# Pooled attention into a mixture-of-depths layer: stores on ScalarE's queue, exponentials in token order, and batch 0's dense work moved ahead of batch 2

## Chip, cores and metric

One Trainium2 chip, one core. The time is device microseconds of one execution of the whole program. Engines are called TensorE (PE, with PEld for its weight loads), VectorE (DVE), ScalarE (ACT), GpSimd (POOL) and SyncE (SP); SP only issues DMAs in this kernel.

## What is computed

Eight batches, eight heads, 576 tokens, head dimension 64. Keys and values are averaged over groups of 8 tokens, so each token attends to 72 pooled keys. The heads side by side give x with 512 columns. A gate score per token picks the 128 best tokens of each batch, and only these go through a two-layer network that is added to x.

```python
def _attn_ref(q, k, v):                       # (8, 8, 576, 64)
    k_p = k.reshape(B, H, Sp, pool, D).mean(axis=3)     # pool = 8, Sp = 72
    v_p = v.reshape(B, H, Sp, pool, D).mean(axis=3)
    scores = np.matmul(q, k_p.transpose(0, 1, 3, 2)) / np.sqrt(D)
    attn = softmax(scores)
    return np.matmul(attn, v_p)               # then (B, S, H*D) = x

def _moe_ref(x, w_gate, w1, w2, capacity):    # w1 (512, 1024), w2 (1024, 512), capacity 128
    scores = np.einsum('bsd,d->bs', x, w_gate)
    out = x.copy()
    for b in range(B):
        top_idx = np.argpartition(-scores[b], capacity)[:capacity]
        xe = x[b, top_idx]
        ye = np.maximum(xe @ w1, 0.0) @ w2
        g = 1.0 / (1.0 + np.exp(-scores[b, top_idx]))
        out[b, top_idx] = x[b, top_idx] + g[:, None] * ye
    return out
```

## The kernel before

`direct_path` does all of the work; `general_path` runs afterwards only if a flag says that a softmax sum left its allowed range. The program's order is written out by hand: every engine executes its instructions in the order in which the Python code emits them, and semaphores hold an instruction until its inputs are there and its buffer is free.

**Tiles.** A token's position in a batch is split as 16 groups of 36 (`G`, `TG`). A tile is 64 tokens: 4 positions of each of 16 groups. A batch has 9 tiles, 3 to a *row* of work: row `u` belongs to batch `u // 3`. `q_trans(u)` transposes the queries of a row on VectorE. `scores(u)` fills four PSUM banks on TensorE (32 products, L281) and ScalarE takes the exponential of each bank into `et` (L285). `attend(a)` multiplies with the pooled values for a *chunk*, two tiles in 128 partitions (L294), into a `pA` buffer, of which there are two; column `D` gives the softmax sum and column `D+1` the gate score. `norm(a)` divides on VectorE (L303, L311, L314) into `xs`, which holds two chunks and has two buffers, or `xh` for the last, half-sized columns of a batch. Tiles are numbered through the batches, so with 9 per batch chunk 4 holds the last tile of batch 0 and the first of batch 1.

**Per batch.** `pool_k` and `pool_v` add groups of 8 on GpSimd (L216, L217, L237 to L241), `k_trans` transposes the sums on VectorE (L222 to L228) and `gate_v` reduces the product of pooled values and gate weights (L245). Batch 0 is pooled partly on VectorE. Then comes the routing: `score` (L354 to L358, with five small GpSimd operations), `row_bcast` (L371) which puts all scores on every partition in PSUM, `count` (L382 to L387) which counts larger scores on VectorE, `one_hot` (L394 to L397), and `gather` (L405 to L415): a product that yields token numbers, the index on GpSimd, and an indirect DMA on GpSimd's queue that reads the chosen rows of `out` back from memory. The gather therefore waits for all stores of its batch. `x_trans` transposes the rows (L428) and ScalarE copies them to `xg` (L430); `hidden`, in three parts (L440), and `finish`, in three parts (L452), are the dense products, followed on GpSimd by the sum with x (L454) and, after the third part, an indirect store.

**Order.** `at(u, slot, job)` enters a job in a table, and the loop over `u` runs the slots of a row between attention steps: attend, slot 1, `scores(u + 1)`, the rest of attend, slot 2, norm, `q_trans(u + 2)`, slots 3 to 7. For batch b, with `w = 3(b + 1)`, the routing stands in rows w and w+1, `x_trans` in slot 5 of row w+2, and the six dense parts in slots 4 and 6 of rows w+3 to w+5:

```python
        at(w, 1 if last else 3, row_bcast, b)
        at(w + 1, 5, gather, b, 3)
        at(w + 2, 5, x_trans, b, 2)
        at(w + 3, 4, hidden, b, 0, 2)
        at(w + 5, 6, finish, b, 2, 1)
```

Loads of keys, values and queries run two batches ahead and are issued on SP. So are the stores of x (`store_x`, L331 to L348), one row after their chunk, in the same queue:

```python
            ins = nc.sync.dma_start(out=rows, in_=x)
            others(ins, b, (scat, gath))
```

The output pattern of a full store is `t g (i d)`, with 8 in front, and that of a half-sized one `t g d`, with 4 in front. Constants for routing (`ident`, `before`, `auxb` and others) are made on VectorE by `constants()` in slot 3 of row 0, behind the first normalisation. `bank(i, shape)` names one of four PSUM banks by hand.

Of the kernel before, what the change touches and what calls it, by code (L numbers as in the profile page):

```python
# [48 lines left out]
def direct_path(ctx, tc, q, k, v, moe_w_gate, moe_w1, moe_w2, moe_capacity, out, flag):  # L49
# [20 lines left out]

    nc = tc.nc
# [23 lines left out]
    NCH = B * NT // 2  # L95
# [21 lines left out]

    nc.vector.memset(vraws[0], 0.0)
    nc.gpsimd.memset(vraws[1], 0.0)
# [10 lines left out]
    load_q(0)  # L130
    load_v(0, 0)
# [23 lines left out]
    for t in kts + vps + vraws[2:]:  # L155
        nc.gpsimd.memset(t, 0.0)
    diff = counted("diff", [C, C], [[1, C]], 0, -1)
    part = counted("part", [C, 1], [[0, 1]], 0, 1)
    steps = counted("steps", [C, C // G - 1], [[-G, C // G - 1]], -G, 1)
# [17 lines left out]
    def constants():  # L177
        nc.vector.tensor_scalar(ident, diff, 0.0, None, op0=OP.is_equal)
        nc.vector.tensor_scalar(before[:, NC - 2, :], diff, 0.0, None, op0=OP.is_lt)
        nc.vector.memset(ones, 1.0)  # L180
        nc.vector.memset(one32, 1.0)

        ge, q16, q4, hi = (const.tile([C, n], FT, name=x) for x, n in (
            ("ge", C // G - 1), ("q16", 1), ("q4", 1), ("hi", 1)))
        nc.vector.tensor_scalar(ge, steps, 0.0, None, op0=OP.is_ge, op1=OP.add, accum_out=q16)
        nc.vector.tensor_scalar(q4, q16, 4.0, None, op0=OP.mult)
        nc.vector.scalar_tensor_tensor(hi, q16, -float(G), part, op0=OP.mult, op1=OP.add)
        nc.vector.tensor_scalar(hi, hi, float(TG), None, op0=OP.mult)
        for i, a in enumerate(auxb):
            nc.vector.tensor_scalar(a[:, 0 : NC - 1, 0], numbers, 0.0, hi, op0=OP.mult, op1=OP.add)  # L190
            nc.vector.tensor_copy(a[:, NC - 1, 0:1], hi)
            nc.vector.tensor_scalar(a[:, i : i + NC - 1, 1], numbers, q4, None, op0=OP.add)  # L192
            h = (NC - 1) * (1 - i)
            nc.vector.tensor_scalar(a[:, h, 1:2], q16, float(32 - 4 * i), None, op0=OP.add)
# [10 lines left out]
    def bank(i, shape):  # L205

        return psum.tile(shape, FT, name=f"bank{i}", bufs=1)
# [22 lines left out]
    def pool_v(b, g, eng):  # L230
        x = VR[b, g]
        VP[b] = vps[b % 2]
        h = slice(HG * g, HG * g + HG)
        if eng is nc.vector:
            eng.tensor_reduce(out=VP[b][:, h, 0:D], in_=x.rearrange("p h t d -> p h d t"), axis=AX.X, op=OP.add)
        else:
            eng.tensor_tensor(out=x[:, :, 0:4, :], in0=x[:, :, 0:4, :], in1=x[:, :, 4:8, :], op=OP.add)  # L237
            eng.tensor_tensor(out=x[:, :, 0:2, :], in0=x[:, :, 0:2, :], in1=x[:, :, 2:4, :], op=OP.add)  # L238
            eng.tensor_tensor(out=VP[b][:, h, 0:D], in0=x[:, :, 0, :], in1=x[:, :, 1, :], op=OP.add)

        nc.gpsimd.tensor_tensor(out=x[:, :, 2, :], in0=VP[b][:, h, 0:D], in1=wg[:, h, :], op=OP.mult)  # L241
# [5 lines left out]


# [25 lines left out]
    def scores(u):  # L274
        b = u // NTH
        p = [bank(i, [128, 2, TS * TL]) for i in range(4)]
# [7 lines left out]
        for i in range(4):  # L284
            nc.scalar.activation(ET[u][i], p[i], AF.Exp, scale=exp_scale)  # L285

    def attend(a, heads=range(H)):
        if heads[0] == 0:
            PA[a] = psum.tile([C, 2, 512], FT, name="pA")
        for h in heads:  # L290
            g, n = divmod(h, HG)
            for t in range(2):
                u, i = divmod(2 * a + t, TS)
                nc.tensor.matmul(PA[a][TL * t : TL * t + TL, g, E * n : E * n + E],  # L294
                                 ET[u][h // 2][:, h % 2, TL * i : TL * i + TL], VP[u // NTH][:, h, :],
                                 start=True, stop=True)

    def norm(a):
        o = PA.pop(a)[:, :, 0 : HG * E].rearrange("p g (n d) -> p g n d", d=E)
        rz = rzall[:, a, :].rearrange("p (g n) -> p g n", g=2)  # L300
        if a % NT == 0:
            SS[a // NT] = work.tile([C, NT, H], FT, name="ss")
        nc.vector.reciprocal(rz, o[:, :, :, D])  # L303
        k = a % NT
        if k == NC - 1:
            XS[a] = work.tile([C, 1, DM], FT, name="xh")
        elif k - (k >= NC) in (0, 2, 4, 6):
            XS[a] = work.tile([C, 2, DM], FT, name="xs")
        else:
            XS[a] = XS[a - 1]  # L310
        nc.vector.tensor_tensor(out=XS[a][:, 0 if XS.get(a - 1) is not XS[a] else 1, :].rearrange("p (g n d) -> p g n d", g=2, d=D), in0=o[:, :, :, 0:D],  # L311
                                in1=rzall[:, a, :].rearrange("p (g n one) -> p g n one", g=2, one=1).to_broadcast(
                                    [C, 2, HG, D]), op=OP.mult)
        nc.vector.tensor_tensor(out=SS[a // NT][:, a % NT, :].rearrange("p (g n) -> p g n", g=2),  # L314
                                in0=o[:, :, :, D + 1], in1=rz, op=OP.mult)
# [15 lines left out]
    def store_x(a):  # L331
        def put(b, rows, x):
            ins = nc.sync.dma_start(out=rows, in_=x)
# [3 lines left out]
        b = 2 * (a // NT)  # L337
        k = a % NT
        if k == NC - 1:
            x = XS[a][:, 0, :]  # L340
            for n in range(2):
                put(b + n, out[b + n].rearrange("(g t) d -> t g d", g=G)[32:TG], x[TL * n : TL * n + TL])
        elif XS.get(a - 1) is XS[a]:
            b += k >= NC
            i = (k - 1) % NC if k < NC else k - NC - 1
# [571 lines left out]
```

## Time and profile before

| | |
|---|---|
| median of 3 runs | 268.03 us (267.51 to 274.88) |
| profiled execution, its own time | 272.41 us |
| span of that execution, first to last instruction | 270.6 us |
| mean granted TensorE clock | 0.925 |
| moved by DMA | 46.94 MB, mean 173 GB/s |

| group of instructions | count | mean | busy |
|---|---|---|---|
| scores, TensorE L281 | 768 | 380 ns | 46.6 us |
| attention times values, TensorE L294 | 1152 | 241 ns | 49.0 us |
| `hidden`, TensorE L440 | 512 | 277 ns | 60.5 us |
| `finish`, TensorE L452 | 384 | 311 ns | 60.2 us |
| exponential, ScalarE L285 | 96 | 495 ns | 39.4 us |
| first value sum, GpSimd L237 | 15 | 2354 ns | 35.3 us |
| normalisation, VectorE L311 | 32 | 691 ns | 22.1 us |

The page's first part gives the busy time of each engine, the second cuts the span into 40 slices of 6.77 us: a digit is the busy share in tenths, PEclk the granted TensorE clock in tenths, DMA the mean share of the 16 DMA engines. A table of stages has the length of the stage, then the busy time and the number of instructions for PE, PEld, DVE, ACT and POOL, then the granted clock, the DMA share and GB/s. The chain of waits has start, length and what was waited for. A timeline row has start, length, engine, line, operation, output, inputs and count; engines with a q are the instruction queues of that engine.

### The profile page before, as it was taken

How to read it: one execution, taken by the hardware profiler on the slowest of the kernel's cores; microseconds unless marked ns; L12 is line 12 of the kernel's file. 1: busy time of each engine (PE TensorE's matmuls, PEld its weight loads, DVE VectorE, ACT ScalarE, POOL GpSimd, SP SyncE). 2: the span in 40 equal slices, each digit the busy share in tenths (PEclk: the TensorE clock that was granted, in tenths of full speed). 3: DMA queues.
4: the chain of work that ended last, by engine and by line, in shares of the span. 5: the costliest groups of instructions: out<-in, count | busy, mean ns of one | idle time of the engine just before them, and what ended most of it. 6: DMA issues, size and time to landing. Idle time of an engine off the chain costs nothing.

```text
span 270.6 us, 7289 instructions
## 1 busy us (share of the span) xinstructions
PE 223.3 (83%) x3050; PEld 207.3 (77%) x3050; DVE 137.6 (51%) x387; ACT 66.5 (25%) x162; POOL 155.1 (57%) x193
## 2 busy tenths in 40 slices
PE   0396176680699999999999999999999999999970
PEld 0376165580599799889997998899889999999970
DVE  7859936664064537654755476538554733411000
ACT  2042022211033133323332333223322331212210
POOL 9889706967970229973995299639953103313021
PEclk9999669656589999999999999999999999999995
DMA  7999997876702636686736276831222203301101
GB/s 278 344 354 398 398 354 284 323 274 204 277 13 50 236 88 206 226 263 208 271 65 249 79 217 224 267 95 44 48 71 79 80 18 116 104 2 39 41 0 51
DMA packets 13048, 46.94 MB, mean 173 GB/s; under 512 B 1104, under 2 KB 1104, under 8 KB 10960
## 3 DMA queue, kind: packets, MB, share of 16 engines
q1 hardware_dynamic: 11728, 42.21, 46.1%
q0 software_dynamic: 1280, 4.20, 4.7%
q8 instruction: 26, 0.43, 0.7%
q14 instruction: 14, 0.11, 0.1%
HBM read 34.87 MB, written 11.53 MB: 171 GB/s over the span
## 4 chain that ended last, share of the span: by engine, by line
PE 69%; DVE 13%; DMA 8%; issue 4%; POOL 3%; ACT 0%; POOLq 0%; DVEq 0%
PE bank L452 21%; PE bank L440 18%; PE bank L281 14%; PE pA L294 13%; DMA out_dram<-xs 5%; DVE qt L271 3%; DMA xr<-out_dram,idx 3%; DVE oh L397 2%; PE bank L371 2%; PE bank L428 2%; DVE xs L311 1%; DVE auxb L192 1%; DVE vp L203 1%; PE bank L405 1%; DVE ge L386 1%
## 5 line engine op out<-in xcount | busy, mean ns | idle before, releaser
L281 PE MATMUL bank<-qt,kt 32*128 32x192 f32 x768 | 46.6, 380 | 18.3 <-DVE qt L271 11.7
L440 PE MATMUL bank<-xg,w 128*128 128x128 f32 x512 | 60.5, 277 | 0.0
L452 PE MATMUL bank<-w,ht 128*128 128x176 f32 (+1 forms) x384 | 60.2, 311 | 0.0
L285 ACT ACTIVATE et<-bank 128x384 f32<-128x384 f32 x96 | 39.4, 495 | 81.9 <-PE bank L281 81.9
L440 PEld LDWEIGHTS bank<-xg,w 128*128 128x128 f32 x512 | 58.4, 192 | 0.5 <-ACT et L285 0.5
L452 PEld LDWEIGHTS bank<-w,ht 128*128 128x128 f32 x384 | 55.8, 190 | 0.6
L294 PEld LDWEIGHTS pA<-vp,et 128*64 128x64 f32 x1152 | 42.4, 152 | 15.7 <-issue 14.9
L281 PEld LDWEIGHTS bank<-qt,kt 32*128 32x128 f32 x768 | 38.6, 216 | 20.6 <-POOL sc L168 11.2
L294 PE MATMUL pA<-vp,et 128*64 128x66 f32 x1152 | 49.0, 241 | 6.1 <-DVE rzall L303 4.7
L303 DVE RECIPROCAL rzall<-pA 128x8 f32<-128x8 f32 x36 | 7.5, 207 | 80.3 <-PE pA L294 80.3
L237 POOL TENSOR_TENSOR vraw<-vraw 128x1024 f32<-128x1024 f32 x15 | 35.3, 2354 | 0.9 <-DVE qt L271 0.9
L454 POOL TENSOR_TENSOR y<-y,xr 128x176 f32<-128x176 f32 (+1 forms) x24 | 13.1, 548 | 39.4 <-ACT y L453 39.0
L271 DVE STREAM_TRANSPOSE qt<-qraw 128x512 f32<-128x512 f32 (+1 forms) x48 | 24.5, 551 | 0.0
L442 ACT ACTIVATE ht<-bank 128x384 f32<-128x384 f32 (+1 forms) x24 | 10.9, 456 | 51.9 <-PE bank L440 51.9
L311 DVE TENSOR_TENSOR xs<-pA,rzall 128x512 f32<-128x512 f32 x32 | 22.1, 691 | 1.4 <-DVE rzall L303 0.2
L453 ACT ACTIVATE y<-bank,g 128x176 f32<-128x176 f32 (+1 forms) x24 | 9.7, 403 | 51.2 <-PE bank L452 51.2
L409 POOL TENSOR_SCALAR idx<-tok 128x1 int32<-128x1 f32 x8 | 1.9, 244 | 31.6 <-DVE g L411 31.4
L238 POOL TENSOR_TENSOR vraw<-vraw 128x512 f32<-128x512 f32 x15 | 19.1, 1272 | 1.2
L386 DVE SCALAR_TENSOR_TENSOR ge<-bank,sc,before 128x128 bf16<-128x128 f32 (+3 forms) x40 | 18.2, 498 | 1.6 <-PE bank L371 1.6
L216 POOL TENSOR_TENSOR kraw<-kraw 128x1152 f32<-128x1152 f32 x7 | 18.4, 2634 | 0.1
L362 POOL CAST auxb<-sc 128x5 bf16<-128x5 f32 x8 | 1.6, 202 | 21.1 <-DVE sc L358 10.7
L428 PE MATMUL bank<-ident,xr 128*128 128x128 f32 x32 | 5.3, 292 | 9.2 <-DMA xr<-out_dram,idx 9.2
(85 smaller groups left out, 186.0 us busy)
## 6 DMA issues: line engine op xcount, KB each, us to landing
kraw<-in_k_dram SPq DMA_DIRECT2D x8, 1152.0 KB
qraw<-in_q_dram SPq DMA_DIRECT2D x8, 1152.0 KB
vraw<-in_v_dram SPq DMA_DIRECT2D x16, 512.0 KB
out_dram<-xs SPq DMA_DIRECT2D x16, 512.0 KB
w<-in_moe_w_dram SPq DMA_DIRECT2D x2, 2048.0 KB
vraw<-in_v_dram SPq DMA_DIRECT2D x16, 64.0 KB
out_dram<-xh SPq DMA_DIRECT2D x8, 128.0 KB
wg<-in_moe_w_gate_dram SPq DMA_DIRECT2D x1, 256.0 KB
```

Source lines behind the costliest of these rows:

```text
L216: eng.tensor_tensor(out=x[:, :, 0:2, :], in0=x[:, :, 0:2, :], in1=x[:, :, 2:4, :], op=OP.add)
L237: eng.tensor_tensor(out=x[:, :, 0:4, :], in0=x[:, :, 0:4, :], in1=x[:, :, 4:8, :], op=OP.add)
L238: eng.tensor_tensor(out=x[:, :, 0:2, :], in0=x[:, :, 0:2, :], in1=x[:, :, 2:4, :], op=OP.add)
L271: nc.vector.transpose(out=QT[u][:, :, n : n + m, :].rearrange("p j t c -> p t j c"), in_=x)
L281: nc.tensor.matmul(p[i][:, s, :], KT[b][r, j, s, :], QT[u][r, j, :, G * s : G * s + G], start=(j == 0), stop=(j == 1))
L285: nc.scalar.activation(ET[u][i], p[i], AF.Exp, scale=exp_scale)
L294: nc.tensor.matmul(PA[a][TL * t : TL * t + TL, g, E * n : E * n + E], ET[u][h // 2][:, h % 2, TL * i : TL * i + TL], VP[u // NTH][:, h, :] ...
L311: nc.vector.tensor_tensor(out=XS[a][:, 0 if XS.get(a - 1) is not XS[a] else 1, :].rearrange("p (g n d) -> p g n d", g=2, d=D), in0=o[:, :, ...
L386: nc.vector.scalar_tensor_tensor(x, y, s, m, op0=OP.is_ge, op1=OP.mult, accum_out=CN[b][:, c : c + 1])
L440: nc.tensor.matmul(p[:, n, :], w1[:, d, 128 * f : 128 * f + 128], XG[b][:, d, :], start=(d == 0), stop=(d == DB - 1))
L452: nc.tensor.matmul(p, HT[b][:, f, :], w2[:, f, c], start=(f == 0), stop=(f == FB - 1))
L454: nc.gpsimd.tensor_tensor(out=Y[b][:, c], in0=Y[b][:, c], in1=XR[b][:, c], op=OP.add)
```

## The change

Nine edits are made together.

1. `store_x` issues on ScalarE's queue instead of SP's, and the output patterns have the 16 groups in front (`g t (i d)`), in two stores of 64 partitions for a pair of chunks.
2. The exponential writes its result in another order of columns, so that the 64 rows of a tile come out group by group. The token numbers in `auxb` are computed for that order by `tokens()`.
3. The tiles of batches 0 and 1 no longer share a chunk: chunk 4 becomes two half-filled chunks (`CH`), 37 chunks in all. `score(0)` moves to row 2, slot 3.
4. Batch 0's routing is entered in rows 3 and 4 and its `x_trans` in row 5, slot 1; its six dense parts follow in row 5, and `scores(6)` for batch 2 stands after the fourth of them. Batch 1's routing runs in row 5, its dense parts in rows 6 to 10; batch 2's in rows 11 to 14. From batch 3 on the rows are as before.
5. `q_trans(u + 2)` stands at the head of row `u` instead of after its normalisations. `scores(1)` moves from ahead of the loop into row 0.
6. The routing constants are made on GpSimd, ahead of the loop, but for one sum on VectorE. Three `vraw` buffers are cleared on ScalarE instead of GpSimd.
7. Batch 0's values are summed on VectorE in three adds for each half.
8. `row_bcast` uses a `pA` buffer, and the other PSUM banks rotate. `count` adds its parts in one reduction.
9. The load of w2 moves to row 2, slot 3, and `k_trans` of batches 1 and 2 to slot 1.

```diff
-    nc.gpsimd.memset(vraws[1], 0.0)
...
     load_k(0)
     load_q(0)
+    for t in vraws[1:]:
+        nc.scalar.memzero(t.rearrange("p h t d -> p (h t d)"))
     load_v(0, 0)
     load_v(0, 1)
...
-    for t in kts + vps + vraws[2:]:
+    for t in kts + vps:
         nc.gpsimd.memset(t, 0.0)
...
-    def constants():
-        nc.vector.tensor_scalar(ident, diff, 0.0, None, op0=OP.is_equal)
...
+    nc.gpsimd.tensor_scalar(ident, diff, 0.0, None, op0=OP.is_equal)
+    nc.gpsimd.tensor_scalar(before[:, NC - 2, :], diff, 0.0, None, op0=OP.is_lt)
...
+    def tokens():
+        nc.vector.tensor_scalar(steps, steps, 0.0, None, op0=OP.is_ge, op1=OP.add, accum_out=q4)
+        nc.gpsimd.tensor_tensor(out=hi, in0=q4, in1=n64, op=OP.subtract)
...
+    turn = [0]
+    def bank(shape, i=None):
+        if i is None:
+            i = turn[0]
+        turn[0] = (i + 1) % 4
         return psum.tile(shape, FT, name=f"bank{i}", bufs=1)
...
     def pool_v(b, g, eng):
-        if eng is nc.vector:
-            eng.tensor_reduce(out=VP[b][:, h, 0:D], in_=x.rearrange("p h t d -> p h d t"), axis=AX.X, op=OP.add)
-        else:
-            eng.tensor_tensor(out=x[:, :, 0:4, :], in0=x[:, :, 0:4, :], in1=x[:, :, 4:8, :], op=OP.add)
+        eng.tensor_tensor(out=x[:, :, 0:4, :], in0=x[:, :, 0:4, :], in1=x[:, :, 4:8, :], op=OP.add)
...
...
+    CH = []
+    for i in range(B * NT // 2):
+        if i == NT // 2:
+            CH += [(2 * i, None), (None, 2 * i + 1)]
+        else:
+            CH.append((2 * i, 2 * i + 1))
...
-            nc.scalar.activation(ET[u][i], p[i], AF.Exp, scale=exp_scale)
+            nc.scalar.activation(ET[u][i].rearrange("p s (n g t) -> p (s n) t g", n=TS, t=QT4),
+                                 p[i].rearrange("p s (n t g) -> p (s n) t g", n=TS, t=QT4), AF.Exp, scale=exp_scale)
...
     def store_x(a):
         def put(b, rows, x):
-            ins = nc.sync.dma_start(out=rows, in_=x)
+            ins = nc.scalar.dma_start(out=rows, in_=x)
...
-            x = XS[a].rearrange("p i d -> p (i d)")
-            y = out[b].rearrange("(g t) d -> g t d", g=G)[:, 0:32].rearrange("g (t i) d -> t g i d", i=4)
-            put(b, y[:, :, i : i + 2, :].rearrange("t g i d -> t g (i d)"), x)
+            y = out[b].rearrange("(g t) d -> g t d", g=G)[:, 0:32].rearrange("g (t i) d -> g t i d", i=4)
             for n in range(2):
+                put(b, y[:, QT4 * n : QT4 * n + QT4, i : i + 2, :].rearrange("g t i d -> g t (i d)"),
+                    XS[a][TL * n : TL * n + TL].rearrange("p i d -> p (i d)"))
...
     def row_bcast(b):
-        SR[b] = [bank(0, [C, NC - 1, C]), bank(1, [C, 1, C])]
+        p = psum.tile([C, 2, 512], FT, name="pA")
...
+            at(*((u + 1, 2) if u != 5 else (u, 5)), store_x, a)
...
+        for f in (score, parts):
+            at(*((w - 1, 3) if b % 2 or b == 0 else (w, 1)), f, b)
+        steps_of = {
+            0: dict(row_bcast=(3, 0), one_hot=(3, 4), gather=(4, 1), x_trans=(5, 1),
+                    dense=((5, 2), (5, 4), (5, 5), (5, 7), (5, 9), (5, 11))),
+            1: dict(row_bcast=(5, 4), one_hot=(5, 6), gather=(5, 8), x_trans=(6, 5),
+                    dense=((6, 6), (7, 4), (8, 4), (9, 4), (9, 6), (10, 4))),
+            2: dict(row_bcast=(9, 3), one_hot=(10, 3), gather=(10, 5), x_trans=(11, 3),
+                    dense=((11, 4), (11, 6), (12, 4), (13, 4), (13, 6), (14, 4))),
+            B - 1: dict(row_bcast=(w, 1), one_hot=(w, 7), gather=(w + 1, 5), x_trans=(w + 2, 5)),
+        }.get(b, dict(row_bcast=(w, 3), one_hot=(w + 1, 3), gather=(w + 1, 5), x_trans=(w + 2, 5)))
+        dense = steps_of.get("dense", [(w + 3 + i // 2, 4 + 2 * (i % 2)) for i in range(6)])
...
-            at(u + 1, 3, k_trans, b + 1)
+            at(*((u + 1, 1) if b < 2 else (u + 1, 3)), k_trans, b + 1)
...
-    at(1, 0, lambda: nc.sync.dma_start(out=w2, in_=moe_w2.rearrange("(a p) n -> p a n", p=128)))
+    at(5, 8, scores, NTH * 2)
+    at(2, 3, lambda: nc.sync.dma_start(out=w2, in_=moe_w2.rearrange("(a p) n -> p a n", p=128)))
     eights()
-    pool_v(0, 0, nc.gpsimd)
+    tokens()
     pool_k(0, nc.vector)
     k_trans(0)
     q_trans(0)
     scores(0)
+    pool_v(0, 0, nc.vector)
+    pool_v(0, 1, nc.vector)
     q_trans(1)
-    scores(1)
-    pool_v(0, 1, nc.vector)
     gate_v(0, 0)
     gate_v(0, 1)
-    at(0, 3, constants)
     for u in range(NU + 6):
+        if u + 2 < NU:
+            q_trans(u + 2)
         run(u, 0)
...
-        if 0 < u < NU - 1:
+        if u < NU - 1 and u != NTH * 2 - 1:
             scores(u + 1)
...
-        if u + 2 < NU:
-            q_trans(u + 2)
-        for slot in range(3, 8):
+        for slot in range(3, 13):
             run(u, slot)
```

## Prediction

> **What bounds the kernel now.** I read the page's slices first (is one engine full, and where not), then busy time by stage, then the chain of waits through the part that isn't full, then the timeline at its longest pieces. Engine totals, then the slices (one digit each 6.77 us):
>
> ```profile
> PE 223.3 (83%) x3050; PEld 207.3 (77%) x3050; DVE 137.6 (51%) x387; ACT 66.5 (25%) x162; POOL 155.1 (57%) x193
> ...
> PE   0396176680699999999999999999999999999970
> ...
> PEclk9999669656589999999999999999999999999995
> DMA  7999997876702636686736276831222203301101
> ```
>
> ```profile
> 30.00:45.00 15.00, 10.75 (x181) 9.41 (x181) 8.59 (x26) 3.28 (x8) 4.14 (x9) 0.70 0.93 340
> 45.00:59.00 14.00, 8.05 (x124) 7.22 (x124) 11.28 (x31) 1.67 (x4) 12.91 (x11) 0.66 0.87 315
> 59.00:72.00 13.00, 3.79 (x64) 3.12 (x62) 2.75 (x9) 2.31 (x6) 9.19 (x11) 0.63 0.70 250
> ...
> 99.40:126.50 27.10, 26.54 (x398) 24.77 (x398) 16.23 (x47) 8.11 (x20) 20.21 (x27) 1.00 0.66 208
> 126.50:153.50 27.00, 26.36 (x370) 24.21 (x369) 14.78 (x42) 8.11 (x20) 18.32 (x17) 1.00 0.57 186
> ```
>
> Two regimes. From 72 to 260 us TensorE (first busy column) does 26.5 of each 27 us: one batch per period, nothing to gain but less work. From 30 to 72 us it does 22.6 of 42 us, at a granted clock near 0.66. The chain names what stands there:
>
> ```profile
> 22.71 1.29 DVE ident L178
> ...
> 26.91 2.24 DVE auxb L192
> ...
> 30.07 13.98 DMA out_dram<-xs
> ...
> 55.42 1.27 POOL vraw L238
> ...
> 58.47 3.45 issue
> 61.92 8.24 DMA xr<-out_dram,idx
> ```
>
> These are VectorE's constants (22.6 to 29.2) ahead of a normalisation, a store that lands 14 us late behind loads on SP's queue and holds its `xs` buffer, and batch 0's gather, asked for at 61.9 and landed at 70.2, on which TensorE stands with nothing else in its order. Its first dense product starts at 77. Two rows of the timeline are needed below: a load [...], and GpSimd reaching a gather's index only after a value sum.
>
> ```profile
> 16.44 8.59 SPq L110 DMA_DIRECT2D kraw<-in_k_dram  x1
> ...
> 115.55 0.28 PE L405 MATMUL bank<-auxb,oh 128*128 128x5 bf16 x5 [0.56 <-DVE oh L397]
> ...
> 117.66 0.68 POOL L241 TENSOR_TENSOR vraw<-vp,wg 128x256 f32<-128x256 f32 x1
> ...
> 118.43 0.25 POOL L409 TENSOR_SCALAR idx<-tok 128x1 int32<-128x1 f32 x1
> ```
>
> [...] The old output pattern has 8 (full) or 4 (half columns) in front, the new one 16. [...] a store in the loads' queue took 13.98 us, gathers on their own queue 3.4 to 8.2. [...] the 8.59 us row shows how long one issue can last. [...]
>
> **The change, part by part.** Anchor: the row's scores at 72.39 start the full stretch; from there to the span's end is 270.6 - 72.39 = 198.2 us. If batch 0's transpose `x_trans` starts at T after the change, the work left is the same plus what before had already done: scores of row 6 (1.55), the rest of batch 1's attention (1.1 + 0.6) and `x_trans` (0.45), 3.7 in all. New span = T + 201.9 + new stalls. The tail after 207 us keeps its order.
>
> *To T.* Batch 1's queries lie behind 7.34 MB in SP's queue. By the GB/s slices (278, 344, 354, then 398) that is through at 22.2 us; value half (0,0), 2.95 MB, was through at 9.9 and used at 11.15, so 1.2 is added: 23.4. `q_trans(3)` now heads row 1 on VectorE, so all behind it waits for that. Behind it stand four normalisations at 1.05 (207, 691 and 150 ns), `k_trans(1)` 2.1, `q_trans(4)` 1.0, a gate reduction 0.4, `score(0)` 0.3: 8.0 + 1.0 for itself, so batch 0's scores are there at 32.4. Its own chunk 4 alone costs one more normalisation, counted. Constants no longer stand here (6.5 us gone).
>
> GpSimd then: batch 1's pooling ends at about 32 as before (17.48 to 32.06; its start waits for the key load, about 17). Its constants, some 20 ops at 0.15 to 0.25 = 4 us, fit where 1.8 + 3.6 us of memsets leave. Next in its order: `parts(0)` 1.3, `pool_k(2)` 4.1, `pool_v(2,0)` 5.1, index 0.3: the gather's issue at 43.3, though its matmul is ready near 40. It is the value sum of batch 2 that is late next, not the store: the last store of batch 0 is issued near 38 on ScalarE's own queue and 5 us suffice. Landing: 4.3 is the median, 8.2 was measured under load; loads of batch 3 and w2 fill the queue here (19.8 MB to move, at 0.39 MB/us until about 54). I take 6.3, between them: T = 49.6 (47.6 to 51.5).
>
> *New stalls.* (a) `hidden(0,0)` follows `x_trans(0)` directly, so the 0.59 copy is bare: 0.7. (b) `row_bcast(1)` and `one_hot(1)` have only `hidden(0,2)`, 1.85, between them, and `count` takes 3.2: 1.4. (c) `x_trans(2)` moves up to (11,3), and batch 1's `finish` parts to rows 9 and 10. On GpSimd, counted from the end of `finish(1,0)`: 0.8 to its y sum, `pool_v(4,0)` 5.1, y 0.6, `pool_v(4,1)` 5.1, y 0.6, scatter 1.1, index 0.5, landing 4.3 = 18.1. On TensorE meanwhile: 2.6 + 1.1 + 1.55 + 0.5 + 2.2 + 0.3 + 1.1 + 1.55 + 1.1 = 12.0. Stall 6.1 (1 if GpSimd runs ahead better than I order it). Sum 8.2.
>
> Span = 49.6 + 201.9 + 8.2 = 259.7, against 270.6: 10.9 less. The profiled execution took 272.4 (1.8 outside its span), so 261.5; it was 4.4 above the median of the runs, 268.0, so 257.1 there.
>
> *At nothing.* ScalarE issues 40 stores of 0.64 = 26 us where 24 stood on SP; they come after a row's exponentials, and relu is due 3.5 us after the scores end, exps plus two issues take 2.9. Without that cover: 0.6 a row over 24 rows, 14 us. SP, freed of waits for VectorE (66 us at L333), loads earlier; memory is not the end's path after 54. Exponential in token order: bounds 0 and double (495 ns each, 47 us of ScalarE over 24 rows, 1.64 to 3.3 a row); [...] so 0; 5 us of dense work follow most scores anyway. No faster than now. Memzero on ScalarE: [...] the load that needs the first was issued at 4.6. First value sums on VectorE: by the 1.36 us add of 1152 about 2.3 each, ended near 15.8 against 16.8; hidden by the query load. Row sums in a `pA` buffer: the buffer is held through `count`, under 5.4 us of dense products.
>
> **Rivals.**
> - *A, the forecast*: TensorE fills from about 50 and is held at x_trans(2): 257. For it: the full stretch is the same work. Chance 0.58.
> - *B, the gathers come in time*: T = 47.6 and stall (c) at 1: span 252.6, median 250. For it: a lone gather landed in 3.4 to 4.3. Against: GpSimd does 20 of 22 us per batch while rows carry only 1.33 dense parts. 0.20.
> - *C, the saving is used up*: dense work waits for its gather or w2 until T = 57: 264.5. For it: DMA share 0.9 in all of that stretch, and more loads now run ahead. Against: the gather has its own queue. 0.13.
> - *D, slower, ScalarE held by its stores*: [...] a store issue on ScalarE lasts like the 8.59 us row; exponentials stand behind it, and TensorE behind these. It needs 10.9 + 5.4 lost to be slower by 2%, that is two such waits of 8.1 in TensorE's path; three make 257 + 24 less 5 of cover, 276. For it: SP now issues without pauses and its queue is full until 54. Against: SP waits for buffers (its `v` loads on gate reductions near 30)[...]. 0.09.
>
> **How the numbers follow.** Likeliest: 257. A alone spans 252 to 262 (T and c at their ends). B starts at 248 and C ends near 266; leaving D and a rim out gives 248 to 265. The measurement tells about 2%, 5.4 us, from no change. Faster: A, B and a little of C, 0.78; same: most of C, 0.14; slower: 0.08.
>
> **What would show it.** Right: `x_trans(0)` near 50 with TensorE idle some 5 us before it; GpSimd's first gather directly after a value sum of batch 2; stores landing within 5 us; no VectorE work on `ident` in the chain; a gap of about 6 us before the transpose of batch 2 near 112; from the fourth batch on 27 us a period; the tail unchanged. Wrong: ScalarE's store issues of over 2 us in the first 60, exponentials above 600 ns, TensorE below 9 in slices after 55 us elsewhere, or `x_trans(0)` later than 55.

## The result, and the profile after

The change makes the kernel slower. Its median is 276.24 us (273.28 to 276.35, 4 runs) against 267.86 us for the kernel before (267.51 to 274.88, 4 runs): a ratio of 1.0285, 95% interval 1.0212 to 1.0359. The prediction was 257.0. The kernel before has times near 268 and times near 276 in every group of runs below (none of the latter was profiled), so ratios are taken over the undisturbed executions of both kernels, and where no ratio is given the text names medians.

The profiled execution of the changed kernel took 273.28 us, with a span of 271.5; that of before took 272.41 with 270.6. The two traces have almost the same length although the medians differ by 8, because one execution lies 3 below its median and the other 4.4 above. Differences of stages are read from the traces, the sum from the medians.

First the page: engine totals, three rows of the slices (6.79 us each) and the group of the exponential.

```profile
PE 222.8 (82%) x3050; PEld 206.2 (76%) x3050; DVE 126.6 (47%) x380; ACT 104.4 (38%) x165; POOL 151.9 (56%) x207
...
PE   0359786398878999917999989999999999999970
...
PEclk9999997979999999975999999999999999999995
DMA  7999999999444098260931882033012314301101
...
L307 ACT ACTIVATE et<-bank 128x384 f32<-128x384 f32 x96 | 71.5, 908 | 59.2 <-PE bank L303 56.9
```

TensorE does the same work (222.8 against 223.3), VectorE 11 us less. ScalarE does 38 us more: 32 in its 96 exponentials, at 908 ns instead of 495, and 5.5 in the clears of `vraw` that it has taken over. In the slices the old hole at 30 to 72 us is nearly filled, and two new dips stand in the seventh and eighth slice and in the eighteenth, with a lower clock in them or just behind (0.80 from 45 to 59 us, 0.86 from 99.4 to 126.5). The stages, with the same limits as before:

```profile
30.00:45.00 15.00, 10.31 (x189) 8.95 (x191) 12.22 (x39) 5.91 (x8) 11.58 (x14) 0.96 0.90 296
45.00:59.00 14.00, 9.49 (x109) 8.25 (x104) 3.88 (x12) 3.99 (x7) 6.55 (x6) 0.80 1.03 383
59.00:72.00 13.00, 11.59 (x140) 10.80 (x137) 6.82 (x25) 2.61 (x6) 2.25 (x8) 1.00 0.73 260
99.40:126.50 27.10, 19.10 (x291) 17.31 (x286) 13.27 (x46) 10.84 (x17) 19.42 (x24) 0.86 0.56 197
126.50:153.50 27.00, 26.45 (x364) 24.54 (x365) 13.15 (x40) 11.53 (x18) 17.22 (x18) 0.95 0.53 181
```

From 30 to 72 TensorE is busy for 31.4 us instead of 22.6: 8.8 gained. From 99.4 to 126.5 it is busy for 19.1 instead of 26.5: 7.4 lost again. The chain of waits names what stands at both places, and at a third between them:

```profile
45.05 7.76 DMA xr<-out_dram,idx
52.95 0.64 PE bank L463 x4
53.61 0.59 ACT xg L465
54.25 4.42 PE bank L475 x24
...
79.97 0.98 ACT et L307 x2
80.95 0.42 issue
81.37 0.88 ACT et L307
82.25 0.44 ACT xg L465
82.72 2.94 PE bank L475 x24
...
119.25 4.02 DMA xr<-out_dram,idx
123.41 1.10 PE bank L463 x4
124.53 0.60 ACT xg L465
125.17 7.46 PE bank L475 x48
```

Batch 0's gather lands at 52.8 (70.2 before). Near 80, TensorE stands behind the exponentials of a row and a copy queued behind them. At 119 it stands for batch 2's gather, and the 48 products after it take 7.46 us, where 48 such products take 5.36 later in the same trace. `row_bcast` of batch 4 begins at 157.88 against 157.50 before, and that of batch 6 at 211.65 against 211.23: two batches in 53.8 us in both kernels. So in these two executions all that the change gained at the start was spent before 158 us, and the steady part is the same.

### The profile page after: what moved, and what is told of

Read it like the earlier page. It is cut to its first block, busy times and chain, and to the rows that moved or that the text cites. A ratio compares the mean times of both kernels' runs of the same rounds, so it can differ in the third digit from the quotient of the medians.

```text
span 271.5 us, 7326 instructions
## 1 busy us (share of the span) xinstructions
PE 222.8 (82%) x3050; PEld 206.2 (76%) x3050; DVE 126.6 (47%) x380; ACT 104.4 (38%) x165; POOL 151.9 (56%) x207
## 4 chain that ended last, share of the span: by engine, by line
PE 61%; POOL 11%; DVE 9%; ACT 7%; DMA 6%; issue 3%; POOLq 0%; ACTq 0%
PE bank L475 22%; PE bank L487 18%; PE bank L303 10%; PE pA L318 8%; ACT et L307 6%; DMA xr<-out_dram,idx 4%; POOL vraw L247 3%; POOL kraw L229 2%; DMA kraw<-in_k_dram 2%; DVE ge L421 2%; POOL vraw L248 1%; DVE qt L293 1%; PE bank L463 1%; POOL y L489 1%; POOL out_dram L491 1%
## 5 line engine op out<-in xcount | busy, mean ns | idle before, releaser
L307 ACT ACTIVATE et<-bank 128x384 f32<-128x384 f32 x96 | 71.5, 908 | 59.2 <-PE bank L303 56.9
L475 PE MATMUL bank<-xg,w 128*128 128x128 f32 x512 | 64.4, 286 | 4.3 <-ACT xg L465 3.2
L475 PEld LDWEIGHTS bank<-xg,w 128*128 128x128 f32 x512 | 61.8, 201 | 5.9 <-ACT xg L465 4.1
L318 PEld LDWEIGHTS pA<-vp,et 128*64 128x64 f32 x1152 | 40.7, 141 | 16.3 <-issue 6.8
L303 PE MATMUL bank<-qt,kt 32*128 32x192 f32 x768 | 43.3, 359 | 11.5 <-POOL auxb L202 11.1
L303 PEld LDWEIGHTS bank<-qt,kt 32*128 32x128 f32 x768 | 35.1, 201 | 13.4 <-POOL lo L200 11.1
L331 DVE RECIPROCAL rzall<-pA 128x8 f32<-128x8 f32 (+1 forms) x37 | 7.5, 204 | 71.3 <-PE pA L318 71.2
L247 POOL TENSOR_TENSOR vraw<-vraw 128x1024 f32<-128x1024 f32 x14 | 33.2, 2370 | 0.0
L421 DVE SCALAR_TENSOR_TENSOR ge<-pA,sc,before 128x128 bf16<-128x128 f32 (+3 forms) x40 | 18.4, 505 | 3.1 <-PE pA L405 3.1
L463 PE MATMUL bank<-ident,xr 128*128 128x128 f32 x32 | 5.4, 295 | 11.0 <-DMA xr<-out_dram,idx 10.1
L251 POOL TENSOR_TENSOR vraw<-vp,wg 128x256 f32<-128x256 f32 x16 | 11.5, 716 | 5.0 <-DMA wg<-in_moe_w_gate_dram 2.8
```

Of the source, the lines that this page charges most:

```text
L303: nc.tensor.matmul(p[i][:, s, :], KT[b][r, j, s, :], QT[u][r, j, :, G * s : G * s + G], start=(j == 0), stop=(j == 1))
L307: nc.scalar.activation(ET[u][i].rearrange("p s (n g t) -> p (s n) t g", n=TS, t=QT4), p[i].rearrange("p s (n t g) -> p (s n) t g", n=TS, t ...
L421: nc.vector.scalar_tensor_tensor(x, y, s, m, op0=OP.is_ge, op1=OP.mult, accum_out=k[:, c, 0:1])
L475: nc.tensor.matmul(p[:, n, :], w1[:, d, 128 * f : 128 * f + 128], XG[b][:, d, :], start=(d == 0), stop=(d == DB - 1))
```

## Experiments

### The order of the exponential's columns

Theory S: the write with a step of four numbers (16 bytes) is what doubles the exponential, and it costs time on the path. Rival: the slower exponential is hidden, and the loss has another cause. Four kernels: the change without the step; the kernel before with it; and two other ways to the same order of columns. The first two leave out the matching order of the output rows, which then stand in the wrong places.

```diff
 e1 (changed kernel; rows in the old order)
-            nc.scalar.activation(ET[u][i].rearrange("p s (n g t) -> p (s n) t g", n=TS, t=QT4),
-                                 p[i].rearrange("p s (n t g) -> p (s n) t g", n=TS, t=QT4), AF.Exp, scale=exp_scale)
+            nc.scalar.activation(ET[u][i], p[i], AF.Exp, scale=exp_scale)
 e2 (kernel before, rows in the new order): the same lines the other way round
 e3 (changed kernel): the exponential as in e1, and the order taken by TensorE from the queries
+                    nc.tensor.matmul(p[i][:, s, :].rearrange("p (n g t) -> p n g t", n=TS, t=QT4), KT[b][r, j, s, :],
+                                     QT[u][r, j, :, G * s : G * s + G].rearrange("r (n t) g -> r n g t", t=QT4),
 e4 (changed kernel): the loop's order swapped, so that the step is in the PSUM read
+            nc.scalar.activation(ET[u][i].rearrange("p s (n g t) -> p (s n) g t", n=TS, t=QT4),
+                                 p[i].rearrange("p s (n t g) -> p (s n) g t", n=TS, t=QT4), AF.Exp, scale=exp_scale)
```

> The changed kernel with one edit: the exponential writes its columns in the order in which it reads them, without a step. Rows of the output stand in other places for that; the work is otherwise the same. Theory S (the exponential's stepped write doubled it, 495 to 908 ns, and that delay costs the gain): exponentials back near 495 ns, ScalarE busy some 65 to 70 us, no dense product waiting for an exponential, time 262 to 268 (8 to 14 below the changed kernel). Theory R (the new order of rows and stores on ScalarE's queue cost it, the exponential is hidden): time 273 to 277, exponentials at 495 all the same.

> The kernel before with one edit: the exponential writes with a step of four numbers, as in the changed kernel. Rows of the output stand in other places for that. Theory S: exponentials about 908 ns, ScalarE busy about 106 us; in the full stretch five us of dense products hide it, in rows 0 to 6 up to 1.3 us a row and bank waits come through, time 272 to 280. Theory R: within 2 us of before, 266 to 270.

> The changed kernel with the token order taken into the scores' products: TensorE reads the transposed queries with a step, so that the exponential reads and writes without one; the same result. If a stepped moving operand costs TensorE nothing in four-byte numbers: 32 products stay at 1.51 us a row, exponentials near 495 ns, time as the kernel with the plain exponential (theory S 262 to 268, theory R 273 to 277). If it costs, the 32 products take 2 to 3 us a row, 24 rows, and the time is 12 to 36 us above that.

> The changed kernel with the token order taken by the exponential's read: it reads PSUM with a step of 16 numbers and writes without one; the same result. If only the stepped write was slow: exponentials near 495 ns and time as with the plain exponential. If the step costs on either side: exponentials near 900 ns or more, time 274 to 280.

| kernel | median us (range) | to before, 95% | exponential |
|---|---|---|---|
| e1, no step | 270.23 (270.01 to 270.48) | 1.0049 (0.9974 to 1.0123) | 496 ns |
| e2, before with the step | 283.74 (276.82; 282.48 to 285.39) | none given | 905 ns |
| e3, step in TensorE's read | 293.73 (292.22 to 295.5) | 1.0925 (1.0813 to 1.1037) | 496 ns |
| e4, step in the PSUM read | 269.85 (268.4 to 271.62) | 1.0037 (0.994 to 1.0134) | 496 ns |

The group of e4's exponential and the scores' and exponential's groups of e3, from the tables of groups:

```profile
L307 ACT ACTIVATE et<-bank 128x384 f32<-128x384 f32 x96 | 39.4, 496 | 63.8 <-PE bank L303 59.1
```

```profile
L303 PE MATMUL bank<-qt,kt 32*128 32x192 f32 x768 | 71.4, 511 | 11.4 <-POOL auxb L202 11.3
...
L308 ACT ACTIVATE et<-bank 128x384 f32<-128x384 f32 x96 | 39.5, 496 | 88.4 <-PE bank L303 88.3
```

The same 384 numbers take 908 ns when the step is in the SBUF write and 496 ns when it is in the PSUM read, with a step of 16 numbers there. On TensorE's side the step costs more: in e3 the score products take 511 ns each instead of 360 (there the step is 32 numbers), 28 us of TensorE, which is the engine that bounds. e2's shortest execution is 9.0 us above the shortest of before beside it (267.8), its longest 8.6 above the longest (276.75). Without the stepped write the changed kernel is 6.0 to 6.4 us faster (e1, e4 against 276.24). The traces show where: in the list of TensorE's waits those for `et` are 6.6 us in all in the changed kernel, 0.8 in e4 and in e1. So theory S holds for its part. It isn't all: e4 does all of the changed kernel's work without the stepped write and stands at 270, 13 above the forecast. The runs below look for that part, and all but e12, e15 start from e4.

### Whether the distance is real: the changed kernel again

> The changed kernel itself, beside the same runs of the kernel before as the others of this group. Theory 'the stepped write costs 6': 274 to 277. Rival 'the earlier distance between this kernel and the one with the order on the PSUM side was one of chips': 270 to 272.

277.0 us (275.89 to 277.94), ratio 1.0277 (1.0214 to 1.034), beside runs of before in another group than the first. Each ratio is to before in the same group of runs, and both of this kernel's (1.0285, 1.0277) lie clear of e4's interval (0.994 to 1.0134). So the first theory holds: the 6 to 7 us between this kernel and e4 aren't a matter of chips. In this execution the 24 products after the exponentials near 84 us took 5.49 us, in the first profile 2.94.

### The forecast's own conversion: the kernel before again

> The kernel before, unchanged, for a second profile and more times. The prediction took its sum from one execution of 272.4 and subtracted 4.4 to reach the median of 268.0. Theory 'the spread lies in the start': the executions of 268 and of 272 to 277 differ in the first 75 us (the store that lands late, the gather of batch 0), which the change removes, so that a part of the 10.9 us saved was never in the median. Rival: they differ by a granted clock spread over the whole span, and the saving counts for all.

269.29 us (268.5 to 269.74); the profiled execution took 268.5 with a span of 266.6. Its chain of waits at the gather of batch 0:

```profile
61.31 3.85 DMA xr<-out_dram,idx
65.16 0.14 issue
65.29 1.09 PE bank L428 x4
...
67.46 2.87 PE bank L281 x32
```

In the execution that the prediction read, the gather was asked for at 61.92, took 8.24, and the row's scores began at 72.46. Here it took 3.85 and they began at 67.46. From there to the span's end it is 199.1 us here and 198.1 there. The spans differ by 4.0 us; the execution here is 5.0 ahead at the row's scores, in the stretch that the change replaces, and loses 1.0 behind them. So the first theory holds for these two; for longer executions it is not shown.

### Who makes the gathers late

In e4, `x_trans(0)` starts at 53.92 and `x_trans(2)` at 123.78, with 7.0 and 6.9 us of waiting. GpSimd's timeline of e4, at the two gathers:

```profile
42.32 0.24 POOL L444 TENSOR_SCALAR idx<-tok 128x1 int32<-128x1 f32 x1
46.74 1.23 POOL L448 DMA_INDIRECT xr<-out_dram,idx  x1 [4.18 <-issue]
...
116.65 0.68 POOL L251 TENSOR_TENSOR vraw<-vp,wg 128x256 f32<-128x256 f32 x1
...
119.27 0.24 POOL L444 TENSOR_SCALAR idx<-tok 128x1 int32<-128x1 f32 x1
119.79 1.06 POOL L448 DMA_INDIRECT xr<-out_dram,idx  x1 [0.28 <-POOL idx L444]
```

Two different causes. Batch 0's index is there at 42.56, and the gather is issued 4.2 us later. By the kernel's order it waits for the last stores of its batch; this trace names no releaser, but in e6's the wait before the gather (1.22 us) ends when the half-sized store lands. Batch 2's index has its sum from VectorE at 114.0 (L442) but is made at 119.27, behind two value sums of batch 4.

```diff
 e5: value sum (4,0) in an earlier slot
-            at(u, 5, pool_v, b + 1, 0, nc.gpsimd)
+            at(u, 2 if b == 3 else 5, pool_v, b + 1, 0, nc.gpsimd)
 e6: w2 behind gather(0), held by a one-column write
-    at(2, 3, lambda: nc.sync.dma_start(out=w2, in_=moe_w2.rearrange("(a p) n -> p a n", p=128)))
+    at(4, 1, lambda: nc.gpsimd.memset(w2[:, 0, 0:1], 0.0))
+    at(4, 1, lambda: nc.sync.dma_start(out=w2, in_=moe_w2.rearrange("(a p) n -> p a n", p=128)))
 e7: e5 and e6.  e8: e7, and gate entered ahead of x_trans
 e9: both value sums of batch 4 behind gather(2)
+            at(*((u + 1, 6) if b == 3 else (u, 5)), pool_v, b + 1, 0, nc.gpsimd)
+            at(*((u + 1, 6) if b == 3 else (u + 1, 2)), pool_v, b + 1, 1, nc.gpsimd)
+            at(u + 2, 7 if b == 3 else 2, gate_v, b + 1, 0)
+            at(u + 2, 7 if b == 3 else 3, gate_v, b + 1, 1)
 e11: e9, w2 as in e6, gate as in e8
```

> The changed kernel with the token order taken on the PSUM side (the exponential writes its row without a step), and pool_v(4,0) moved from slot (9,5) to (9,2), so that GpSimd has it behind it when gather(2) is due. Theory 'GpSimd order': x_trans(2) waits 6.9 us in the kernel without this edit because gather(2) is issued at 119.8, behind what GpSimd has ahead of it; with the pooling earlier the wait falls to 2 us or less, the 2 us of hidden products at the half clock (7.5 against 5.4) go with it, time 262 to 264. Rival 'the gather is late for another reason' (its indices, or its transfer of about 4 us): the wait stays above 5 and the time at 268 to 271.

269.54 us (269.18 to 273.31). A miss of mine: the sum was moved, but it still stands ahead of gather(2). GpSimd begins `pool_k` only when the routing of batch 2 has its scores (near 100 us), and does the same work between there and the gather, which is issued at 117.89; TensorE still waits 7.0 us at it.

> The changed kernel with the token order taken on the PSUM side, and the w2 load moved behind the issue of gather(0) (a tiny write of w2 by GpSimd, issued after the gather, holds the load and the loads queued behind it). Theory 'the loads crowd the stores and the gather': without w2 in front, the batch-0 stores land in about 5 us instead of 10, gather(0) is issued near 42.5 instead of 46.7 and lands in 4.5 instead of 7.1, x_trans(0) starts at 47 to 48 instead of 53.9; time 262 to 265. Rival 'the store takes its 10 us by itself': x_trans(0) stays at 52 to 54, time 268 to 271. Price that can turn it: w2 is late for the first y product.

268.88 us (268.32 to 270.14). The local forecast came true: gather(0) issued at 43.9, `x_trans(0)` at 47.7 instead of 53.9. With w2 and the loads behind it held back, the gather is issued 2.9 us earlier than in e4, and TensorE starts on its rows 3.8 us after the issue instead of 7.2. In e4, where these loads run, the busy share of the DMA engines was 1.01 from 45 to 59 us. The time fell by 1.0 only, and the ranges overlap. Batch 1's gather, which was early enough in e4, is now late: `x_trans(1)` waits and starts at 76.4 (of 6.2 us saved 5.7 are left), `x_trans(2)` at 120.6 (3.2), the end 2.4 earlier in the profiled executions.

> Both edits: pool_v(4,0) earlier and the w2 load behind gather(0). If the two waits stand one behind the other on TensorE the savings add: 254 to 258. If the time removed at one is given back at the other (the DVE and GpSimd work near 153 to 158 that stands behind batch 2), it stays at the better of the two, 262 to 265.

> As e7, with gate entered ahead of x_trans as in the kernel before. Theory 'the gate's move costs': the reciprocal on VectorE no longer stands behind the scatter's GpSimd work, 0 to 2 us less than e7. Rival: the gate was off the path, same as e7 within 0.5.

269.61 us (268.72 to 269.87) and 269.24 us (267.68 to 270.43). Neither adds to e6: e7 because e5's edit did nothing, e8 because the gate was off the path. The medians of e7 and e8 are 0.4 apart.

> The changed kernel with the token order taken on the PSUM side, and both value sums of batch 4 (pool_v(4,0), pool_v(4,1)) moved behind gather(2), their gate reductions behind x_trans(2). Theory 'GpSimd order': in the kernel without the edit the index of gather(2) has its sum from VectorE at 114.1 and is made only at 119.3, since GpSimd has 10 us of value sums ahead of it; with them behind it the gather is issued near 114.4 and lands at 118.4, TensorE's 6.9 us wait at x_trans(2) falls to about 1.5 and its next 48 products run at the full clock (5.4 instead of 7.5). 269.9 less 5.4 less 2.1 = 262 to 263. Rival 'given back later': the value sums are late for row 12, TensorE waits there as long, 268 to 270.

272.68 us (268.56 to 274.75), inconclusive as a time. The trace is of an execution of 274.40, one of the two longer ones of four:

```profile
114.90 0.25 POOL idx L444
...
115.43 4.29 DMA xr<-out_dram,idx
119.72 0.14 issue
119.86 1.10 PE bank L463 x4
...
121.62 7.94 PE bank L475 x48
...
132.69 9.70 DMA out_dram<-xs
```

The index is made 4.4 us earlier and `x_trans(2)` starts 3.9 earlier. But the products after it still take 7.94 us, and at 132.7 a store lands 9.70 us late and holds VectorE, whose `oh` TensorE then waits 2.8 us for. Whether that late store belongs to the edit is not shown: e11, with the same edit, waits 1.0 us for `oh`. GpSimd's order was the cause of the late gather, as the first theory says: half of the wait went with it, 3.4 us of 6.9 are left. Taking it away alone is not shown to gain, and the rival's late value sums don't show in this trace.

> The w2 load behind gather(0), gate ahead of x_trans, and both value sums of batch 4 behind gather(2), with the token order taken on the PSUM side. If the savings seen at x_trans(0) (about 5 us of which 3 are given back at x_trans(1)) and at x_trans(2) (about 7) add: 259 to 262. If the wait only moves on to the next gather, 266 to 269.

266.9 us (264.29 to 270.01), the first version below 268, but short of the 259 to 262 of plain addition. Its chain shows the next wait, batch 1's gather, and the slow products after it:

```profile
67.04 9.47 DMA xr<-out_dram,idx
76.50 0.14 issue
76.64 1.10 PE bank L463 x4
...
78.45 5.49 PE bank L475 x24
```

### What a wait costs besides itself

Behind the waits for gathers TensorE's products took longer: in the changed kernel, e4 and e11, after 3.3 to 6.9 us of idle time, 4.42 to 5.49 us for 24 instead of 2.94, and 7.00 to 7.54 for 48 instead of 5.36. Extra transposes of the identity, overwritten by the real ones, were put in the wait: 22 (e10) and 48 (e13) ahead of `x_trans(0)` and `x_trans(2)` in e4; 38 and 24 ahead of `x_trans(1)` and `x_trans(2)` in e11 (e14).

```diff
+        for i in range({0: 48, 2: 48}.get(b, 0)):
+            nc.tensor.transpose(p[:, i % DB, :], ident, ident[:cap, :cap])
         for d in range(DB):
             nc.tensor.transpose(p[:, d, :], XR[b][:, 128 * d : 128 * d + 128], ident[:cap, :cap])
```

> The changed kernel with the token order taken on the PSUM side, and 22 extra transposes of the identity (6 us of TensorE work whose result is overwritten) put ahead of x_trans(0) and of x_trans(2), where TensorE waits 7 us for a gather. Theory 'the wait is paid twice, once as idle time and once in the clock that is granted after it': the first 24 products after x_trans(0) take 2.9 instead of 5.5 and the 48 after x_trans(2) take 5.4 instead of 7.5; 269.9 less 4.7 = 265. Rival 'the slow clock has another cause' (the products are slow because of their operands or the memory traffic): same times of these groups, 270 to 271.

> As e10, with 48 extra transposes instead of 22 ahead of x_trans(0) and x_trans(2): at 119 ns each 5.7 us of the 6.4 to 6.7 us that TensorE waits there. Theory 'the wait is paid twice': with under 1.5 us of idle time left the clock stays full, the 24 products after x_trans(0) take 2.9 instead of 5.3 and the 48 after x_trans(2) 5.4 instead of 7.3; 4.3 us less than without, 265.5. Rival 'another cause': these groups keep their times, 270 to 272.

> e11 (w2 load behind gather(0), gate ahead of x_trans, value sums of batch 4 behind gather(2), token order on the PSUM side) with 38 extra transposes ahead of x_trans(1) and 24 ahead of x_trans(2), where it still waited 5.2 and 3.4 us. If the clock stays full: 24 products 5.5 to 2.9 and 48 products 7.0 to 5.4, 4.2 us less than e11, 262 to 263. Rival: as e11, 266 to 267.

TensorE's timelines at `x_trans` and the products behind it: e10 at batch 0, e13 at batch 2, e14 at batches 1 and 2. The bracket is the idle time before the row.

```profile
52.45 1.12 PE L465 MATMUL bank<-ident,xr 128*128 128x128 f32 x4 [4.11 <-DMA xr<-out_dram,idx]
54.24 5.30 PE L477 MATMUL bank<-xg,w 128*128 128x128 f32 x24 [0.68 <-ACT xg L467]
```

```profile
122.54 0.66 PE L465 MATMUL bank<-ident,xr 128*128 128x128 f32 x4 [1.47 <-DMA xr<-out_dram,idx]
123.87 7.25 PE L477 MATMUL bank<-xg,w 128*128 128x128 f32 x48 [0.68 <-ACT xg L467]
```

```profile
79.18 0.60 PE L465 MATMUL bank<-ident,xr 128*128 128x128 f32 x4
80.51 2.94 PE L477 MATMUL bank<-xg,w 128*128 128x128 f32 x24 [0.73 <-ACT xg L467]
...
116.99 0.66 PE L465 MATMUL bank<-ident,xr 128*128 128x128 f32 x4 [0.56 <-DMA xr<-out_dram,idx]
118.32 5.62 PE L477 MATMUL bank<-xg,w 128*128 128x128 f32 x48 [0.68 <-ACT xg L467]
```

e10: 271.78 us (269.9 to 272.7). The 22 transposes ran in 2.6 us, over 4 us of idle time was left, and the 24 products kept their 5.30 us: undecided. e13: 268.94 us (265.73 to 272.63, 20 runs; the profiled one took 270.14), ratio 0.9941 (0.9901 to 0.9981), against 1.0037 (0.994 to 1.0134) for e4. The 24 products of batch 0 went from 5.49 to 4.57, but the 48 of batch 2 kept 7.25, though only 1.47 and 0.68 us of idle time were left: the theory fell short of its size there. The granted clock was 0.51 from 124 to 127 us and back at 1.00 from 128. e14 decides. With 0.73 us of idle time or less in front, the 24 products take 2.94 instead of the 5.49 of e11, and with 0.56 and 0.68 the 48 take 5.62 instead of 7.00. The products and their operands are those of e11; the work put into the wait is what differs. The stretches of these products, first e11's two and then e14's, have the granted clock, the DMA share and GB/s as their last three columns:

```profile
78.45:83.94 5.49, 5.49 (x26) 5.26 (x28) 0.00 (x0) 0.00 (x0) 5.25 (x5) 0.50 0.22 91
119.05:126.05 7.00, 7.00 (x48) 6.81 (x48) 0.84 (x5) 0.49 (x1) 6.03 (x7) 0.79 0.00 0
```

```profile
80.51:83.45 2.94, 2.94 (x26) 2.82 (x28) 0.00 (x0) 0.00 (x0) 2.70 (x4) 1.00 0.69 292
118.32:123.94 5.62, 5.62 (x48) 5.43 (x48) 0.00 (x0) 0.49 (x1) 5.38 (x5) 1.00 0.00 0
```

The slow products ran at a granted clock of 0.50 and 0.79 and the fast ones at 1.00, and memory traffic is not the cause: it was higher beside the fast 24, and absent beside both groups of 48. Where e14 has no extra work, at `x_trans(0)`, TensorE waited 2.89 us and the 24 products took 4.96; in e11 it waited 0.26 there and they took 2.94. In these traces the slow products are part of the price of a wait: 2.55 us behind e11's at `x_trans(1)`, 1.38 behind that at `x_trans(2)`.

e14 is also the version that beats both: 264.39 us (263.07 to 266.25, 6 runs), ratio to before 0.9821 (0.9767 to 0.9876), and 12.6 below the changed kernel in the same group. Against e11's median, from another group, it is 2.5 less, where 4.2 had been expected; the ranges overlap, so the gain is shown for the products and not for the whole time.

### The stores' queue by itself

```diff
-            ins = nc.scalar.dma_start(out=rows, in_=x)
+            ins = nc.sync.dma_start(out=rows, in_=x)
```

> The changed kernel with the token order taken on the PSUM side, and the stores back on SP's queue, behind the loads. Theory 'the queue of their own is what brings batch 0's gather forward': stores of batch 0 stand behind loads that wait for buffers, gather(0) is issued 10 us or more later, x_trans(0) at 60 to 66 instead of 53.9 and the time 276 to 282. Rival 'the memory is what they wait for, whichever the queue': x_trans(0) at 52 to 56, time within 2 of 270.

280.45 us (278.98 to 281.21), ratio 1.0401 (1.0338 to 1.0463). The time is in the first theory's range, the place only in part. The wait at `L463` in the list of TensorE's waits (total, times, longest):

```profile
PE bank L463 <- DMA xr<-out_dram,idx: 22.4, 2, 12.8
```

`x_trans(0)` starts at 56.95, 3 us later than in e4 and not 6 to 12; the longest wait, 12.8, is that of batch 2, whose `x_trans` starts at 132.60 (123.78 in e4). There the gather is issued 3.0 us later than in e4 (122.75) and takes 9.71 us to land; why it takes so long stays open. A queue of their own for the stores is worth about 10 us to this schedule (280.45 less 269.85), more of it later than I had thought.

## Why the prediction was wrong

The forecast was 257.0; the changed kernel takes 276.2, e4 269.9. Three terms of the sum were mis-sized, one of them put at nothing, and a fourth was missing.

1. **"Exponential in token order: ... so 0."** It costs 6.4 us (276.24 less 269.85), in the kernel before about 9 (e2). Of the two ends I had named, 0 and double, the measured one is 1.83 times, 908 against 495 ns. I took the lower end, and nothing had shown it: in the trace of before no exponential writes with a step. The measurement decides: for ScalarE's write this step isn't free. The cover I claimed ("5 us of dense work follow most scores") wasn't enough either: the trace has TensorE behind `et` at five lines, 6.6 us in all, and the copy of `xg` behind four exponentials near 82 us. It also pushed the start: the last stores of batch 0 are issued from 37.65 here, in e4 from 35.52.

2. **"it was 4.4 above the median of the runs, 268.0, so 257.1 there."** This 4.4 was taken off a time in which it was no longer contained. The sum replaced the start of the profiled execution with T. e12 shows that the profiled execution was late exactly there (gather 8.24 us against 3.85). The sum should have stopped at 261.5.

3. **"T = 49.6".** It was 52.95, and 53.92 in e4. The order of GpSimd's work was right, the index came at 44.50 (43.3 forecast; its terms add to 43.2), and in e4 at 42.32. What was too small is the memory's share: "5 us suffice" for the last store, but in e4 it is issued at 36.81 and the gather that waits for it at 46.74; and 6.3 for the gather's landing, which took 7.76 in the changed kernel and 7.05 in e4, at DMA shares of 1.03 and 1.01 from 45 to 59 us. e6 shows that it is the loads: with w2 behind the gather T is 47.7. That puts e4's start 4.3 us behind the forecast. Not all of it need reach the end: e6 took 6.2 off T, and its time fell by 1.0, while the next gather came late.

4. **The clock after a wait, which has no term at all.** The wait at `x_trans(2)` was forecast at 6.1 "near 112" and is 6.8 and ends at 123.4, at the named place and from the named cause. But the products behind it take 7.5 instead of 5.4, and those behind `x_trans(0)` 5.5 instead of 2.9 in e4: 4.7 us more. The trace of before had a sign of it, a granted clock near 0.66 from 30 to 72 us, where TensorE was busy for 22.6 of 42 us, and I had the number in hand without pricing it. How short a pause is enough is not shown: in e13 the clock was at 0.51 after 1.47 and 0.68 us with 0.66 us of work between, in e14 at 1.00 after 0.56 and 0.68.

Together: 257.0 + 4.4 + 4.3 + 4.7 = 270.4 for e4. The execution that the last two terms are read from took 271.62, e4's median is 269.85. The 6.4 of the first term is itself the distance from e4 to the changed kernel, so adding it tests nothing; the runs without the stepped write and the waits for `et` do. The sum says where the time stood, not what would come back if a term were taken away: in e14's trace `x_trans(0)` starts at 47.42, earlier than forecast, the step is gone and two waits are filled, and its median, 264.4, is still 3 us above the 261.5 at which the sum should have stopped. Those 3 us stay open.

Right were: TensorE filling the stretch from 30 to 72; the first gather directly behind a value sum of batch 2; the constants gone from the chain; 27 us a batch later on, with the same tail; and the stall at batch 2's gather. Rival D's time, 276, is what came, but not by its mechanism: the store issues on ScalarE took 0.55 to 1.75 us up to 60 us, none near 8. Rival C, gathers delayed by loads that run ahead, names the cause that e6 confirms for the late start, with T at 57 where 53 to 54 was measured. Two of the signs that I had listed as "wrong" were decisive, exponentials above 600 ns and a dip of TensorE after 55 us. No run changes the stores' output pattern alone, so whether 16 groups in front helped is not shown; nor were edits 3 to 8 tried one by one.

## What to carry to other kernels

Price a change of layout at the end of the instruction that carries it: here the same reordering was free in a PSUM read by ScalarE (496 ns against 495), cost 6 us as an SBUF write (908 ns) and 24 us in TensorE's operand (511 ns a product against 360). Price a wait on TensorE as the wait plus the slow products behind it: in e11 5.18 us and 2.55 more at `x_trans(1)`. A wait taken away at one place came back here at the next one, with slow products behind it (24 took 5.49 us in e6 and in e11). Work that filled it kept the clock though its result was thrown away (1.00 in e14 against 0.50 and 0.79 in e11). When a forecast replaces a stage of a profiled execution, ask whether this execution's distance from the median lies in that stage before taking it off again.

## What the runs showed of the hardware

- ScalarE writing 128x384 fp32 to SBUF with a step of 16 bytes: 904 to 908 ns against 495. Reading the same from PSUM with a step of 64 bytes: 496.
- TensorE reading its fp32 moving operand with a step of 128 bytes: 511 ns a product against 360 for runs of 16 numbers.
- The granted clock was 0.51 over 3 us after pauses of 1.47 and 0.68 us with 0.66 us of work between them (e13), and stayed at 1.00 after pauses of 0.56 and 0.68 (e14).
- Landing differed between executions: the same gather took 8.24 and 3.85 us in two executions of the kernel before, at a DMA share of 0.70 and 0.71 from 59 to 72 us.
